# Mask passes of 32 rows beside the scores in a routed attention kernel

## The chip, the cores and the metric

The kernel runs on one core of a Trainium2 chip. A core has TensorE (PE in the profile), VectorE (DVE), ScalarE (ACT), GpSimd (POOL) and a queue for transfers (SP). The metric is the device time of one execution in microseconds; here the median of three runs.

## The reference

Two blocks follow each other: attention in which a query sees only the keys of its own cluster, and a two-layer network on the result. Only the first block is touched.

```python
q_assign = np.argmax(np.einsum('bhsd,hcd->bhsc', q_n, c_n), axis=-1)
k_assign = np.argmax(np.einsum('bhsd,hcd->bhsc', k_n, c_n), axis=-1)
mask = q_assign[:, :, :, None] == k_assign[:, :, None, :]
scores = scale * np.matmul(q, k.transpose(0, 1, 3, 2))
scores = np.where(mask, scores, -1000000000.0)
scores = scores - np.max(scores, axis=-1, keepdims=True)
attn = np.exp(scores)
attn = attn / (np.sum(attn, axis=-1, keepdims=True) + 1e-09)
return np.matmul(attn, v).astype(np.float32)
```

Batch 4, 8 heads, 768 tokens, head width 64, 16 clusters. The second block is `(h * erf(softplus(h))) @ w_out` with `h = x @ w_in`, for 3072 tokens, widths 512 and 2048.

## The kernel before

**Pairs, periods, units.** Attention goes through 16 pairs of heads (pair 0 to 15). The two heads `e` of a pair lie in partitions 0 to 63 and 64 to 127, so that two matmuls with 64 rows each work beside each other. A pair has 12 units `u`: two halves of 384 queries, and in each half six blocks of 128 keys. Two units make a period: six periods `i` = 0 to 5 for a pair, the first half in 0 to 2, the second in 3 to 5. `period(p, i)` writes out by hand the order of everything; every engine keeps the program's order (`InOrder`).

**What a unit needs.** `products` writes q times k in f32 into a `sc` bank (two pairs of passes, from `qT` and `kT`, in every third pair from parts of `more_out`). `scores` adds a bf16 pass of `km` and `qm`: the mask, and in one row the negative maximum of each query. `curve` is ACT's exponential from `sc` to `pr`. In the period after, `accumulate` sums `pr` on POOL and `attend` multiplies it with v into `turned[half]` (tile `turned`, 128 rows and 64 columns for each head).

**Masks.** `hotT` holds a one for each token's cluster. `masks(p, nm, half, bank)` multiplies it with the constant `pick`, which puts the 16 cluster rows of head `e` at the rows `e * 64` of a `turned` bank; ACT copies the bank to `qm` (Relu) or `km` (scale 2^60 and bias `nbig`, so that 0 stands where clusters agree and -2^60 elsewhere). The masks of the next pair are made in four places of a period's list (`MASKS`): place 0 after the first maxima step, 1 after the products, 2 after the scores with ACT's copy between the two curves, 3 at the end. Rows in use for a head: 16 cluster rows, and row 32 (`SH`) for the maximum.

**Maxima, half a pair ahead.** `maxima_step` finds the maxima for six units later: a pass of `qv` and `kv` (bf16 copies) into the one tile `wide`, a pass of `qm` and `km` on top, both with 64 rows, then a DVE reduction to `nmx`. A period has two such steps: at its start, and after the products. After every sixth step a small reduction writes `lowest`; at the start of periods 0 and 3 `turn` brings it to rows by six matmuls into `turned`, and ACT copies one row for each head into `qm` (`CAST qm<-turned`), which `scores` of that period reads.

**Other work in the order.** At the end of periods 0 and 3 `divide` multiplies the sums with `minus` on PE and takes `inv` on ACT; in the next period DVE makes `den` and `turned<-turned,inv` after place 0, and `more_out<-den,turned` after place 1, whose result SP stores. ACT makes the bf16 copies `kv` in period 4 and `qv` in period 5. For the second block DVE, ACT and POOL also rearrange weights in pairs 1 to 11 (`size_and_rest`, `bounded`, `sign`, `shifted`, `summed`; `sign` is the int16 `x_own` of the profile, in periods 2 and 4), and from pair 11 on DVE forms sums of weights. `similarities` and `choose`, for the pair after the next, begin in period 3 and end in 5.

The helper `InOrder` issues all instructions, so that nearly every row of the profile has the line L63; tiles tell the rows apart.

Of the kernel before, what the change touches and what calls it, by code (L numbers as in the profile page):

```python
# [20 lines left out]
B, H, S, D = 4, 8, 768, 64  # L21
C = 16
NJ = S // P
Q = 32
# [4 lines left out]
NPAIR = B * HP  # L29
# [14 lines left out]
BIG = 2.0**60  # L44
FLOOR = 2.0**50
EPS = 2.0**-70
SH = 2 * C
NPT = NJ + 2
N_LATE = 10
LAST_X = 11  # L50
MASKS = {(0, 1): ("k", 0), (0, 2): ("k", 1), (2, 0): ("q", 0), (5, 0): ("q", 1)}
FIRST_MASKS = {(2, 0): ("k", 0), (2, 1): ("q", 0), (2, 2): ("k", 1), (5, 0): ("q", 1)}


class InOrder:
# [16 lines left out]
def kernel(  # L72
# [13 lines left out]
    te, ve, ae, ge = (  # L86
        InOrder(tc, e, in_order) for e in (nc.tensor, nc.vector, nc.scalar, nc.gpsimd)
    )
# [8 lines left out]
    turned = [ps.tile([P, 512], F32, name=f"turned{i}") for i in range(2)]  # L97
# [12 lines left out]
    def passing(name, bufs, **kw):  # L110
        return attention.enter_context(tc.tile_pool(name=name, bufs=bufs, **kw))

    ps_s = passing("ps_s", 2, space=PSUM)
    wide = passing("ps_w", 1, space=PSUM).tile([P, 2, 512], F32, name="wide")
# [9 lines left out]
    first = const.tile([P, P], BF16, name="first")  # L124
    pick = const.tile([P, 2, P], BF16, name="pick")
    nbig = const.tile([P, 1], F32, name="nbig")
    ccT = const.tile([P, HP, 2 * C], F32, name="ccT")

    lowest = [const.tile([P, HJ, P], BF16, name=f"lowest{i}") for i in range(2)]
# [11 lines left out]
    rows = [{nm: const.tile([P, S], F32, name=f"{nm}T{i}") for nm in "qk"} for i in range(2)]  # L141
# [56 lines left out]
    for base, pattern, sign, op, fill in (  # L198
# [5 lines left out]
            out=first, in_=first, compare_op=op, fill=fill, base=base, pattern=pattern,  # L204
# [23 lines left out]
    steps = {}  # L228
# [29 lines left out]

    ve.memset(nbig, 0.0)
    for e in range(2):  # L260
        ve.memset(nbig[e * D : e * D + C], -BIG)
        ve.memset(nbig[e * D + SH : e * D + SH + 1], 1.0)
    for t in maxima:
        ve.memset(t, FLOOR)
    ve.memset(pick, 0.0)
# [81 lines left out]
        if p < NPAIR:  # L347
            ae.copy(out=pairs[p][nm + "v"], in_=pairs[p][nm + "T"])

    def masks(p, nm, half, bank):  # L350

        if p >= NPAIR:
            return lambda: None
        st = pairs[p]
        cols = slice(half * HW, (half + 1) * HW)
        r = slice(0, D) if nm == "q" else slice(D, P)
        won = bank[:, 0:HW]
        te.matmul(won, lhsT=pick[r, half], rhs=st["hotT"][r], start=True, stop=True)
        if nm == "q":
            return lambda: ae.activation(out=st["qm"][:, cols], in_=won, func=ACT.Relu)  # L360
        return lambda: ae.activation(
            out=st["km"][:, cols], in_=won, func=ACT.Identity, bias=nbig, scale=BIG
        )

    turns = []

    def maxima_step(p, i, sm=wide):

        st = pairs[p]
        nmx = maxima[p % 2]  # L370
        t, half = divmod(i, 2)
        for a, b, start in (("qv", "kv", True), ("qm", "km", False)):
            for e in range(2):
                r = slice(e * D, (e + 1) * D)
                te.matmul(
                    sm[:, e, 0:HW], lhsT=st[a][r, t * P : (t + 1) * P],
                    rhs=st[b][r, half * HW : (half + 1) * HW], start=start, stop=not start,
                )
        ve.tensor_reduce(
            out=nmx[:, :, t, half], in_=sm[:, :, 0:HW], axis=AX.X, op=ALU.max, negate=True  # L380
        )
        if i in (NJ - 1, 2 * NJ - 1):
            h = i // NJ
            ve.tensor_reduce(
                out=lowest[h][:, :, SH::D].rearrange("p t e -> p e t"),
                in_=nmx[:, :, h * HJ : (h + 1) * HJ], axis=AX.X, op=ALU.min,
            )
            turns.append((p, h))

    def turn(p, h, copies=(ae.copy, ae.copy)):  # L390

        st = pairs[p]
        pn = turned[h][:, 0:HW].rearrange("p (t n) -> p t n", t=HJ)
        for t in range(HJ):
            for e in range(2):
                cols = slice(e * D, (e + 1) * D)
                te.matmul(pn[cols, t], lhsT=lowest[h][:, t, cols], rhs=identb, start=True, stop=True)
        for e, copy in zip(range(2), copies):
            r = slice(e * D + SH, e * D + SH + 1)
            copy(out=st["qm"][r, h * HW : (h + 1) * HW], in_=pn[r].rearrange("p t n -> p (t n)"))  # L400
        st["shift", h] = True

# [20 lines left out]
    def scores(u):  # L423

        p, half, j = units[u]
        st = pairs[p]
        sc = sc_of[u]
        assert ("shift", half) in st
        for e in range(2):
            r = slice(e * D, (e + 1) * D)  # L430
            te.matmul(
                sc[:, e, 0:HW], lhsT=st["km"][r, j * P : (j + 1) * P],
                rhs=st["qm"][r, half * HW : (half + 1) * HW], start=False, stop=True,
            )
# [270 lines left out]
    def run(work):  # L705
        for _ in work:
            pass

    def step_ahead(u):
        p, i = divmod(u + NJ, 2 * NJ)
        if p < NPAIR:
            maxima_step(p, i)

    forms = sum((left_forms(ve, *w_in_parts(f, 2)) for f in range(0, HF, 2)), [])
    routing = [iter(())]
# [2 lines left out]
    def period(p, i):  # L720
        u = 2 * NJ * p + 2 * i
# [3 lines left out]
        def mask(place):  # L725
            which = (MASKS if p else FIRST_MASKS).get((i, place))
            if which:
                return masks(p + 1, *which, turned[0 if i in (0, 5) else 1])
            return lambda: None

        if u > 0:
            for which in turns if i in (0, 3) else ():
                turn(*which)
                turns.remove(which)
            step_ahead(u)
# [4 lines left out]
        products(u)  # L740
        products(u + 1)
        mask(1)()
        if u > 0:
            step_ahead(u + 1)
        next(part[0], None)
        scores(u)
        scores(u + 1)
        later = mask(2)
        if i == 3:
# [65 lines left out]
    def warm(n, bank, rhs):  # L815
        for _ in range(n):
            te.matmul(bank[:, 0 : rhs.shape[-1]], lhsT=identb, rhs=rhs, start=True, stop=True)
# [9 lines left out]
    for e in range(2):  # L827
        ve.tensor_copy(
            out=ccT[e * D : (e + 1) * D, :, e * C : (e + 1) * C],
            in_=pct[e * D : (e + 1) * D].rearrange("d (r e c) -> d r e c", e=2, c=C)[:, :, e],  # L830
# [7 lines left out]
    for r in (0, D):  # L838
        for half in range(2):
            for e in range(2):  # L840
                c = r + half * Q + e * C
                ve.tensor_copy(
                    out=pick[r : r + D, half, e * D : e * D + C], in_=first[r : r + D, c : c + C]
                )
    also = ps_s.tile([P, 2, 512], F32, name="sc", tag="s")
    products(0)
# [11 lines left out]
    for n in range(PLACES - 1):  # L858
        fetch(n)
    for i in range(NJ):  # L860
        maxima_step(0, i, also if i % 2 else wide)
        if i == 1:
            masks(0, "q", 1, turned[1])()
        if i < NJ - 1:
            warm(2, turned[0], zeros)
    step_ahead(0)
    warm(2, turned[0], zeros)
    turn(0, 0, (ae.copy, ve.tensor_copy))
    turns.clear()
    transposes(1, "k")  # L870
# [12 lines left out]
    u = len(units)  # L883
# [107 lines left out]
```

## Time and profile before

| what | value |
| --- | --- |
| median of three runs | 1022.77 us (1022.52 to 1022.77) |
| the execution profiled | 1022.77 us, of it span 1021.1 us from the first to the last instruction |
| granted TensorE clock | 1.00 |
| first `kv` pass, last score pass of the attention | 12.1 us, 433.6 us |
| PE busy from 50 to 400 us | 349.75 of 350.00 us |
| DVE, ACT, POOL busy from 50 to 400 us | 264.19, 266.40, 259.88 us |
| pair 8, period 1, `kv` to `kv` | 233.51 to 237.33 us |
| reduction `nmx<-wide` | 189 times, median 959 ns |
| ACT copies `qm<-turned` of 384 columns, 128 rows | 31 times, median 490 ns |
| ACT copies `km<-turned` | 32 times, mean 578 ns |

A row of the timeline gives start and duration in microseconds, engine, line, operation, output and inputs, rows times columns of a matmul's weights, shapes and number of instructions; idle time before it and who ended that stand in brackets. A matmul's duration includes its way through the array, so that two that follow each other overlap, and the distance of their starts tells the time that one takes.

### The profile page before, as it was taken

The page shows a single profiled execution, that of the slowest core. Times are in us where ns is not written, and L with a number is a line of the kernel's source. Part 1 is how long each engine was busy: PE and PEld are TensorE (multiplying, and loading weights), DVE is VectorE, ACT ScalarE, POOL GpSimd, SP SyncE. Part 2 cuts the span into 40 slices and gives each one's busy share as a digit, 9 for nine tenths or more (in the row PEclk, how much of TensorE's full clock was granted, in tenths as well). Part 3 has the DMA queues.
Part 4 walks back from the last instruction along what each step waited for, and adds up shares of the span by engine and source line. Part 5 has one row for each costly group of instructions (what it writes and reads, how often), then busy time and mean ns, then how long its engine had stood idle before and what let it go on. Part 6 is the DMA issues. An engine that isn't in the chain of part 4 may idle for free.

```text
span 1021.1 us, 15464 instructions
## 1 busy us (share of the span) xinstructions
PE 1013.9 (99%) x5930; PEld 726.1 (71%) x5930; DVE 695.8 (68%) x1305; ACT 515.0 (50%) x673; POOL 345.7 (34%) x229
## 2 busy tenths in 40 slices
PE   8999999999999999999999999999999999999998
PEld 3555555554555445478888888888888888888887
DVE  8777777777777777778875674756565547565754
ACT  3787877787777666567615142322233141505050
POOL 1777777777777667745130000000000000000000
PEclk9999999999999999999999999999999999999999
DMA  9344444444343311041100100110011000000001
GB/s 214 68 98 97 104 104 103 104 104 104 83 104 87 76 28 32 24 154 61 42 1 21 63 1 1 42 42 1 1 41 42 1 21 22 1 1 21 21 1 41
DMA packets 141641, 55.55 MB, mean 54 GB/s; under 512 B 127104, under 2 KB 131456, under 8 KB 141568
## 3 DMA queue, kind: packets, MB, share of 16 engines
q1 hardware_dynamic: 139216, 54.28, 20.8%
q8 instruction: 46, 0.75, 0.3%
q10 hardware_dynamic: 2352, 0.30, 0.2%
q14 instruction: 27, 0.22, 0.1%
HBM read 41.98 MB, written 12.58 MB: 53 GB/s over the span
## 4 chain that ended last, share of the span: by engine, by line
PE 97%; DVE 1%; POOL 0%; ACT 0%; issue 0%; DVEq 0%; ACTq 0%; POOLq 0%
PE bank L63 43%; PE turned L63 33%; PE sc L63 15%; PE wide L63 7%; DVE nmx L63 1%; POOL more_out L63 0%; DVE sims L63 0%; ACT inv L63 0%; DVE kT L63 0%; DVE qT L63 0%; ACT pr L63 0%; DVE hotT L63 0%; DVE wide L63 0%; DVE den L63 0%; DVE hot L63 0%
## 5 line engine op out<-in xcount | busy, mean ns | idle before, releaser
L63 POOL TENSOR_TENSOR more_out<-more_out,pr 128x768 f32<-128x768 f32 x128 | 223.5, 1746 | 67.6 <-ACT pr L63 62.5
L63 DVE TENSOR_REDUCE nmx<-wide 128x2 f32<-128x768 f32 x189 | 180.7, 956 | 95.1 <-PE wide L63 70.8
L63 ACT ACTIVATE pr<-sc 128x768 f32<-128x768 f32 x192 | 147.0, 810 | 75.0 <-PE sc L63 75.0
L63 PE MATMUL turned<-pr,in_v 128*64 128x386 f32 x768 | 145.5, 500 | 0.1
L63 DVE TENSOR_TENSOR g<-bank,g 128x256 f32<-128x256 f32 x222 | 89.5, 421 | 52.9 <-PE bank L63 46.3
L63 PE MATMUL bank<-x_own,w_in 128*128 128x256 f32 x424 | 104.5, 380 | 0.0
L63 PE MATMUL bank<-w_out,g 128*128 128x256 f32 x448 | 103.1, 379 | 0.0
L63 PE MATMUL sc<-qT,kT 64*128 64x384 f32 x528 | 99.7, 484 | 0.0
L63 PEld LDWEIGHTS turned<-pr,in_v 128*64 128x64 f32 x768 | 46.7, 136 | 72.2 <-issue 71.1
L63 PEld LDWEIGHTS bank<-w_out,g 128*128 128x128 f32 x448 | 85.2, 190 | 11.5
L63 PEld LDWEIGHTS bank<-x_own,w_in 128*128 128x128 f32 x424 | 80.4, 190 | 12.1 <-issue 1.2
L63 ACT COPY g<-bank 128x256 f32<-128x256 f32 x28 | 10.4, 372 | 152.5 <-PE bank L63 148.5
L63 DVE TENSOR_TENSOR osb<-bank,osb 128x256 f32<-128x256 f32 x87 | 35.4, 420 | 72.8 <-ACT osb L63 25.4
L63 ACT ACT_TABLE_LOAD x48 | 61.6, 1283 | 45.7 <-DVE g L63 45.0
L63 POOL TENSOR_TENSOR more_out<-pr,pr 128x768 f32<-128x768 f32 x32 | 58.8, 1837 | 58.5 <-ACT pr L63 58.5
L63 PE MATMUL bank<-x_more,more_in 128*128 128x256 f32 x296 | 76.0, 379 | 0.0
L63 PEld LDWEIGHTS <-qv 64*128 64x128 bf16 x384 | 25.6, 93 | 65.2 <-issue 51.1
L63 PE MATMUL wide<-kv,qv 64*128 64x384 bf16 x378 | 69.4, 328 | 1.1 <-ACT km L63 0.6
L63 PEld LDWEIGHTS sc<-qT,kT 64*128 64x128 f32 x528 | 56.6, 187 | 16.6 <-issue 1.2
L63 PE MATMUL wide<-km,qm 64*128 64x384 bf16 x378 | 68.3, 322 | 0.0
L63 PE MATMUL bank<-more_out,g_more 128*128 128x256 f32 x272 | 64.3, 379 | 0.0
L63 DVE TENSOR_TENSOR g<-a_s,g 128x512 f32<-128x512 f32 x96 | 62.4, 688 | 1.4 <-ACT a_s L63 1.4
(162 smaller groups left out, 1710.2 us busy)
## 6 DMA issues: line engine op xcount, KB each, us to landing
x_own<-in_moe_w_in_dram SPq DMA_DIRECT2D x13, 512.0 KB, 4.3
in_v<-in_v_dram SPq DMA_DIRECT2D x32, 192.0 KB, 2.9
x_dram<-more_out SPq DMA_DIRECT2D x32, 192.0 KB, 2.4
x_own<-x_dram SPq DMA_DIRECT2D x6, 1024.0 KB, 5.1
out_dram<-osb SPq DMA_DIRECT2D x23, 256.0 KB, 2.0
in_k<-in_k_dram SPq DMA_DIRECT2D x59, 96.0 KB, 2.7
in_q<-in_q_dram SPq DMA_DIRECT2D x58, 96.0 KB, 3.6
g_more<-in_moe_w_out_dram SPq DMA_DIRECT2D x6, 512.0 KB, 3.6
```

What stands on the lines that cost most here:

```text
L63: ins = getattr(self.engine, name)(*args, **kw)
```

## The change

The row of the maximum and the cluster rows move into 17 rows (row 0 the maximum, rows 1 to 16 the clusters), and `pick` writes them twice for each head: at rows 0 to 16 and at rows 32 to 48 of its 64, the second time with 0 for the maximum in `km`. `scores` now reads rows 0 to 31 of each head. `maxima_step` becomes a generator. The first step of a period runs through as before, with 64 rows. The second one stops after its `kv` pass (`behind`), is resumed after `scores(u)`, does its `km` pass with rows 32 to 63 of each head, and then its reduction. `next(part[0])`, the divide's second part, stands between the two. Two masks move: the second half of `k` from place 2 of period 0 to place 2 of period 2, the second half of `q` from place 0 to place 2 of period 5; in pair 0 the former was in that place already. At place 2 their product takes 32 rows of `hotT` and `pick` (`narrow`).

```diff
@@ -44,12 +44,11 @@
 BIG = 2.0**60
 FLOOR = 2.0**50
 EPS = 2.0**-70
-SH = 2 * C
 NPT = NJ + 2
 N_LATE = 10
 LAST_X = 11
-MASKS = {(0, 1): ("k", 0), (0, 2): ("k", 1), (2, 0): ("q", 0), (5, 0): ("q", 1)}
-FIRST_MASKS = {(2, 0): ("k", 0), (2, 1): ("q", 0), (2, 2): ("k", 1), (5, 0): ("q", 1)}
+MASKS = {(0, 1): ("k", 0), (2, 0): ("q", 0), (2, 2): ("k", 1), (5, 2): ("q", 1)}
+FIRST_MASKS = {(2, 0): ("k", 0), (2, 1): ("q", 0), (2, 2): ("k", 1), (5, 2): ("q", 1)}
 
 
 class InOrder:
@@ -258,8 +257,10 @@
 
     ve.memset(nbig, 0.0)
     for e in range(2):
-        ve.memset(nbig[e * D : e * D + C], -BIG)
-        ve.memset(nbig[e * D + SH : e * D + SH + 1], 1.0)
+        for n in range(2):
+            r = e * D + n * Q
+            ve.memset(nbig[r : r + C + 1], -BIG)
+            ve.memset(nbig[r : r + 1], 1.0 - n)
     for t in maxima:
         ve.memset(t, FLOOR)
     ve.memset(pick, 0.0)
@@ -347,13 +348,15 @@
         if p < NPAIR:
             ae.copy(out=pairs[p][nm + "v"], in_=pairs[p][nm + "T"])
 
-    def masks(p, nm, half, bank):
+    def masks(p, nm, half, bank, narrow=False):
 
         if p >= NPAIR:
             return lambda: None
         st = pairs[p]
         cols = slice(half * HW, (half + 1) * HW)
         r = slice(0, D) if nm == "q" else slice(D, P)
+        if narrow:
+            r = slice(r.start + half * Q, r.start + (half + 1) * Q)
         won = bank[:, 0:HW]
         te.matmul(won, lhsT=pick[r, half], rhs=st["hotT"][r], start=True, stop=True)
         if nm == "q":
@@ -364,25 +367,31 @@
 
     turns = []
 
-    def maxima_step(p, i, sm=wide):
+    def maxima_step(p, i, sm=wide, behind=False):
 
         st = pairs[p]
         nmx = maxima[p % 2]
         t, half = divmod(i, 2)
-        for a, b, start in (("qv", "kv", True), ("qm", "km", False)):
+
+        def passes(a, b, start, rows):
             for e in range(2):
-                r = slice(e * D, (e + 1) * D)
+                r = slice(e * D + rows.start, e * D + rows.stop)
                 te.matmul(
                     sm[:, e, 0:HW], lhsT=st[a][r, t * P : (t + 1) * P],
                     rhs=st[b][r, half * HW : (half + 1) * HW], start=start, stop=not start,
                 )
+
+        passes("qv", "kv", True, slice(0, D))
+        if behind:
+            yield
+        passes("qm", "km", False, slice(Q, D) if behind else slice(0, D))
         ve.tensor_reduce(
             out=nmx[:, :, t, half], in_=sm[:, :, 0:HW], axis=AX.X, op=ALU.max, negate=True
         )
         if i in (NJ - 1, 2 * NJ - 1):
             h = i // NJ
             ve.tensor_reduce(
-                out=lowest[h][:, :, SH::D].rearrange("p t e -> p e t"),
+                out=lowest[h][:, :, ::D].rearrange("p t e -> p e t"),
                 in_=nmx[:, :, h * HJ : (h + 1) * HJ], axis=AX.X, op=ALU.min,
             )
             turns.append((p, h))
@@ -396,7 +405,7 @@
                 cols = slice(e * D, (e + 1) * D)
                 te.matmul(pn[cols, t], lhsT=lowest[h][:, t, cols], rhs=identb, start=True, stop=True)
         for e, copy in zip(range(2), copies):
-            r = slice(e * D + SH, e * D + SH + 1)
+            r = slice(e * D, e * D + 1)
             copy(out=st["qm"][r, h * HW : (h + 1) * HW], in_=pn[r].rearrange("p t n -> p (t n)"))
         st["shift", h] = True
 
@@ -428,6 +437,7 @@
         assert ("shift", half) in st
         for e in range(2):
             r = slice(e * D, (e + 1) * D)
+            r = slice(r.start, r.start + Q)
             te.matmul(
                 sc[:, e, 0:HW], lhsT=st["km"][r, j * P : (j + 1) * P],
                 rhs=st["qm"][r, half * HW : (half + 1) * HW], start=False, stop=True,
@@ -708,10 +718,12 @@
 
 
 
-    def step_ahead(u):
+    def step_ahead(u, behind=False):
         p, i = divmod(u + NJ, 2 * NJ)
-        if p < NPAIR:
-            maxima_step(p, i)
+        steps = maxima_step(p, i, behind=behind) if p < NPAIR else iter(())
+        if not behind:
+            run(steps)
+        return steps
 
     forms = sum((left_forms(ve, *w_in_parts(f, 2)) for f in range(0, HF, 2)), [])
     routing = [iter(())]
@@ -725,7 +737,7 @@
         def mask(place):
             which = (MASKS if p else FIRST_MASKS).get((i, place))
             if which:
-                return masks(p + 1, *which, turned[0 if i in (0, 5) else 1])
+                return masks(p + 1, *which, turned[0 if i in (0, 5) else 1], place > 1)
             return lambda: None
 
         if u > 0:
@@ -740,10 +752,11 @@
         products(u)
         products(u + 1)
         mask(1)()
-        if u > 0:
-            step_ahead(u + 1)
+        second = step_ahead(u + 1, True) if u > 0 else iter(())
+        next(second, None)
         next(part[0], None)
         scores(u)
+        next(second, None)
         scores(u + 1)
         later = mask(2)
         if i == 3:
@@ -840,7 +853,8 @@
             for e in range(2):
                 c = r + half * Q + e * C
                 ve.tensor_copy(
-                    out=pick[r : r + D, half, e * D : e * D + C], in_=first[r : r + D, c : c + C]
+                    out=pick[r : r + D, half, e * D : (e + 1) * D].rearrange("p (n c) -> p n c", n=2)[:, :, 1 : C + 1],
+                    in_=first[r : r + D, c : c + C].unsqueeze(1).to_broadcast([D, 2, C]),
                 )
     also = ps_s.tile([P, 2, 512], F32, name="sc", tag="s")
     products(0)
@@ -858,7 +872,7 @@
     for n in range(PLACES - 1):
         fetch(n)
     for i in range(NJ):
-        maxima_step(0, i, also if i % 2 else wide)
+        run(maxima_step(0, i, also if i % 2 else wide))
         if i == 1:
             masks(0, "q", 1, turned[1])()
         if i < NJ - 1:
```

## The prediction

> **What bounds the kernel now.** I read the page first, then the PE's, ScalarE's (ACT) and VectorE's (DVE) parts of the timeline inside single periods of the attention part.
>
> ```profile
> PE 1013.9 (99%) x5930; PEld 726.1 (71%) x5930; DVE 695.8 (68%) x1305; ACT 515.0 (50%) x673; POOL 345.7 (34%) x229
> ```
>
> PE has no idle time to speak of, and the chain of waits gives it 97% of the span. But matmul ends are modelled, so lateness hides in start times. A period without masks, turns or divides before it (pair 8, period 1; the columns are start, duration, engine, line, operation):
>
> ```profile
> 233.51 0.34 PE L63 MATMUL wide<-kv,qv 64*128 64x384 bf16 x2
> ...
> 235.14 0.33 PE L63 MATMUL wide<-kv,qv 64*128 64x384 bf16 x2
> 235.30 0.33 PE L63 MATMUL wide<-km,qm 64*128 64x384 bf16 x2
> 235.46 0.49 PE L63 MATMUL sc<-qm,km 64*128 64x384 bf16 x4
> 235.88 1.52 PE L63 MATMUL turned<-pr,in_v 128*64 128x386 f32 x8
> 237.33 0.34 PE L63 MATMUL wide<-kv,qv 64*128 64x384 bf16 x2
> ```
>
> A pair of bf16 passes (two heads, one beside the other) takes one slot of 0.16 us; the period is 3.82 from `kv` to `kv`. From the second score slot (235.62) to the attend matmuls it is 0.26, not 0.16: 0.10 go with the change of tile shape. At the start 64-row passes at 14.20 are followed by 128-row ones at 14.46, again 0.26, though the columns stay 128. I read this as: a change of rows alone costs about 0.10 too.
>
> Period 0 of pair 9, whose beginning belongs to the turn:
>
> ```profile
> 254.66 0.34 PE L63 MATMUL turned<-identb,lowest 128*64 128x128 bf16 x6
> 254.94 0.34 PE L63 MATMUL wide<-kv,qv 64*128 64x384 bf16 x2
> ...
> 256.57 0.32 PE L63 MATMUL turned<-hotT,pick 64*128 64x384 bf16 x1
> ...
> 257.56 0.32 PE L63 MATMUL turned<-hotT,pick 64*128 64x384 bf16 x1
> 257.81 0.55 PE L63 MATMUL turned<-pr,in_v 128*64 128x386 f32 x2
> ```
>
> The last score pass here starts at 257.22; the second mask comes 0.34 after it, because it writes the bank that ACT is still copying the first mask from.
>
> ```profile
> 253.33 1.51 ACT L63 ACTIVATE pr<-sc 128x768 f32<-128x768 f32 x2 [0.21 <-PE sc L63]
> 254.73 0.83 ACT L63 CAST qv<-qT 128x768 bf16<-128x768 f32 x1
> 255.57 0.95 ACT L63 CAST qm<-turned 1x384 bf16<-1x384 f32 x2
> ...
> 258.19 0.58 ACT L63 ACTIVATE km<-turned,nbig 128x384 bf16<-128x384 f32 x1
> 258.65 0.81 ACT L63 ACTIVATE pr<-sc 128x768 f32<-128x768 f32 x1
> ```
>
> ACT runs from the curves of period 5 without a gap to the turn's two copies, which end at 256.52; the first mask starts at 256.57. **This queue is only just in time.** Between periods 2 and 3 it is late already:
>
> ```profile
> 239.87 1.51 ACT L63 ACTIVATE pr<-sc 128x768 f32<-128x768 f32 x2 [0.96 <-PE sc L63]
> 241.27 1.37 ACT L63 ACTIVATE x_own<-x_own 128x512 int16<-128x512 f32 x1
> 242.67 0.96 ACT L63 CAST qm<-turned 1x384 bf16<-1x384 f32 x2
> ```
>
> The copies end at 243.63, and the four score passes of that period (from 243.43) take 0.74 against the 0.49 above: 0.25 lost. DVE in period 1:
>
> ```profile
> 234.05 0.96 DVE L63 TENSOR_REDUCE nmx<-wide 128x2 f32<-128x768 f32 x1 [1.01 <-PE wide L63]
> 234.93 0.55 DVE L63 SCALAR_TENSOR_TENSOR den<-turned,inv 128x384 f32<-128x384 f32 x1
> 235.39 0.62 DVE L63 SCALAR_TENSOR_TENSOR turned<-turned,inv 128x384 f32<-128x384 f32 x1
> 235.92 0.95 DVE L63 TENSOR_REDUCE nmx<-wide 128x2 f32<-128x768 f32 x1
> 236.78 0.55 DVE L63 SCALAR_TENSOR_TENSOR more_out<-den,turned 128x384 f32<-128x384 f32 x1
> ```
>
> Five instructions back to back; the second reduction ends at 236.87 and frees `wide` for the `kv` at 237.33, 0.46 to spare.
>
> **What PE gains, step by step.** The second maxima step lies in 92 of 96 periods. Its mask pass moves beside the first scores: minus one slot, 0.16. The scores now take 32 rows, so between `kv` (64 rows) and scores there is a new change of shape: +0.10. It is not shown for 64 to 32 rows; bounds are 0 (as between passes of one shape) and 0.15 (scores to attend, 0.10, and 0.05 more of the first attend slot, 0.37 against 0.32). I take 0.10, the row with equal columns: net -0.06 x 92 = -5.5. Four periods have scores but no second step: +0.4. That four row tiles run at once the trace doesn't show, only two; bounds: free, or a whole slot of 0.16. The nearest row are the similarities, four column tiles started within 0.02 us and gone in 0.35, no more than the 0.37 of a two-tile attend slot after its change of shape: I take free.
>
> The Trainium skill, "TensorEngine Tiling (Array Packing)", Key Properties, says that changing the tiling mode drains TensorE; it gives no price. By the rule the change pays at each such border, as in the sum; without it the 92 slots would bring 14.7. Its "TensorE: Matmul & The Clock Gate", section "Measured speedup vs the span model", measured 3.07 times, not 4, for four 32-row tiles; an estimate from that page is a slot longer by a third, 0.05, some +2 us in all.
>
> Masks: in pairs 1 to 14 the second `k` mask leaves period 0, whose 0.34 and whose slot go together (scores to attend would be 0.25 again, against 257.22 to 257.81): -0.34 x 14 = -4.8. It goes beside scores in period 2, as does pair 0's, and the second `q` mask in period 5 of 15 pairs. A mask takes one head's rows alone and shifts it by a slot until the next change of shape: 16 x -0.16 = -2.6. What hides these masks is the second scores slot; without it 30 x 0.16 = 4.8 come back. PE alone: -5.5 + 0.4 - 4.8 - 2.6 = **-12.5**.
>
> **What the queues take.** *DVE, periods 1 and 4.* The change resumes the second step after the divide's last part, so `more_out<-den,turned` goes ahead of the second reduction. It reads the result before it: 235.39 + 0.62 + 0.03 (such a step in the similarity chain, 245.09 + 0.58 to 245.70) = 236.04, that is 2.53 after `kv`. The reduction follows 0.46 later (the spacing of `den`), runs 0.96, and PE needs 0.05 (copies' end to mask): 4.00, against 3.76 by PE alone. Next `kv` late by 0.24; 30 such places (period 1 of 15 pairs, period 4 of 15): +7.2. The reduction also comes 0.15 later against the next period everywhere; elsewhere 0.3 or more remains, except in pairs 12 and 13, where extra DVE sums lie between (there a reduction ends at 348.70 and `kv` starts at 348.75): +0.3.
>
> *ACT, period 5 into 0.* The `q` copy (0.49) was made before the curves, while ACT waited for scores; now it lies between them. From the scores' start: 0.43 to the curve, 1.40 for two curves, 0.39 for the copy (0.49 less the 0.10 by which such instructions overlap), 0.84 `qv`, 0.95 turn copies, 0.05: 4.06. PE reaches the first mask in 0.16 + 0.26 + 1.34 (attends) + 0.28 (turn) + 1.63 = 3.67. Late by 0.39, and second `kv`, scores and the attends are queued behind the mask: 14 x 0.39 = +5.5.
>
> *ACT, period 2 into 3.* The `k` copy is now between those curves (0.46, 258.19 to 258.65), ahead of the weight step `x_own` (1.40) in pairs 1 to 11: 0.43 + 1.40 + 0.46 + 1.40 + 0.96 + 0.05 = 4.70 to the scores of period 3. PE: 2.04 to `kv`, 1.63 + 0.26 to the scores, 3.93. Late by 0.77, of which 0.25 is there now: 11 x 0.52 = +5.7. Behind the scores wait the mask pass, similarities and attends. Without `x_own` the chain is 3.30, nothing late.
>
> *Setup.* Four more small memsets (59 ns each) on DVE and wider `pick` copies, partly under the centroids' load: 0 to 0.4, I take +0.2. No DMA is added; the store of `x` leaves one reduction earlier, SP waits on nothing new. POOL's sums get a later curve by 0.4 in periods 2 and 5, with over 1 us before the divide: nothing.
>
> Sum: -12.5 + 7.2 + 0.3 + 5.5 + 5.7 + 0.2 = **+6.4**. On the execution profiled (span 1021.1, timed 1022.77, which is the median shown): **1029.2 us**.
>
> **Rivals.** *No price from 64 to 32 rows.* Then -0.10, but only where PE decides: periods 1 and 4 wait for DVE, 3 for ACT; left are some 50 places, -5.0: 1024.2. For it: no row shows that border; against: both borders shown cost the same 0.10.
>
> *The change doesn't do what it says: 32-row passes run one after the other.* Then 0.16 per period, hidden again in 1 and 4 (0.24 of slack), and once each in the two ACT chains: some 36 places, +5.8: 1035.0. For: never seen here; against: the four column tiles.
>
> *Faster: ACT swallows the two copies.* One mechanism: between curves they cost ACT's queue nothing, as it idles elsewhere (50% busy, 0.96 idle before the curves of period 2). Then the 11.2 of both chains go: 1018.0. It decides for faster once the copies cost less than 0.37 of their 0.85 per pair. Against: 258.19 to 258.65 shows such a copy holding the next curve by 0.46, and the idle time lies before the curves, where the copy no longer is.
>
> **Numbers.** Forecast 0.64; no price 0.10 (half of it above +0.2%); one after the other 0.14; faster 0.09; something cancelling within 0.2% 0.03. A time within 0.2% (2.0 us) is no change that a measurement here can tell. Faster 0.09, same 0.08, slower 0.83. The forecast's own range is 1026 to 1032 (drain 0.05 to 0.15 in some 50 places); with most of both neighbours 1024.6 to 1034.6.
>
> **What would show it.** After: `kv` to `kv` in periods 1 and 4 about 4.00, with `more_out<-den,turned` ahead of the second `nmx`; scores 0.26 after the second `kv`, the narrow `km` within 0.01 of the scores and the next scores 0.16 on; no mask after the scores of period 0; the first mask there late by 0.4 behind the turn copies; scores of period 3 late by 0.8. Wrong: `kv` to `kv` at 3.76 or less in period 1, or a mask in period 0 that starts 1.63 after `kv`.

## The result, and the profile after

| | median | lowest to highest | runs |
| --- | --- | --- | --- |
| before | 1022.68 us | 1022.52 to 1022.77 | 5 |
| after | 1051.19 us | 1051.17 to 1052.42 | 5 |

The changed kernel takes 1.0281 times as long, with an interval of 1.0269 to 1.0292: **28.5 us slower**, where the prediction had 6.4 and a range that ended at 1034.6. The sign was right, the size was not. The execution profiled is the one of 1052.42 us (span 1050.7), 29.65 above the profile of before.

First the page's busy times and its chain of waits, of the kernel after:

```profile
PE 1009.8 (96%) x5930; PEld 705.2 (67%) x5930; DVE 736.6 (70%) x1309; ACT 511.0 (49%) x673; POOL 342.2 (33%) x229
...
PE 70%; DVE 25%; DMA 3%; issue 1%; ACT 0%; SPq 0%; DVEq 0%
```

The chain of before:

```profile
PE 97%; DVE 1%; POOL 0%; ACT 0%; issue 0%; DVEq 0%; ACTq 0%; POOLq 0%
```

PE has 4.1 us less to do, in a span that is 29.6 longer. VectorE is busy for 40.8 us more, with four instructions more, and its share of the chain that ended last goes from 1% to 25%. Which wait that is, says the list of PE's waits (who waits, for whom, us in all, times, longest), of after:

```profile
PE wide L62 <- DVE nmx L62: 31.0, 60, 1.6
```

and of before:

```profile
PE wide L63 <- DVE nmx L63: 0.4, 2, 0.2
```

Sixty times a `kv` pass waits for a reduction to free `wide`. From the starts of the first `kv` pass of every period, the lengths of the periods of pair 8 (pairs 1 to 11 agree within 0.03 us) against those that the prediction's terms give (period 0: 4.97 - 0.06 - 0.34 + 0.39; period 3: 5.50 - 0.06 + 0.52; period 5: 4.15 - 0.06 - 0.16):

| period | 0 | 1 | 2 | 3 | 4 | 5 |
| --- | --- | --- | --- | --- | --- | --- |
| before | 4.97 | 3.82 | 4.15 | 5.50 | 3.82 | 4.15 |
| predicted | 4.96 | 4.00 | 4.09 | 5.96 | 4.00 | 3.93 |
| after | 5.49 | 4.01 | 4.09 | 6.81 | 4.01 | 3.93 |

Four of six are right to 0.01. Periods 0 and 3 are 0.53 and 0.85 too long. A pair is longer than before by 1.96 us in pairs 1 to 11 (21.5 in all), and by 4.15, 2.46, 0.76 and 1.13 in pairs 12 to 15, mostly in periods 0 and 3 again (in pair 14 in period 3 alone).

The timeline of TensorE after, a period without turns or masks (pair 7, period 4; columns as in the lines of before):

```profile
235.52 0.34 PE L62 MATMUL wide<-kv,qv 64*128 64x384 bf16 x2
235.80 0.34 PE L62 MATMUL sc<-qm,km 32*128 32x384 bf16 x2
235.80 0.33 PE L62 MATMUL wide<-km,qm 32*128 32x384 bf16 x2
235.97 0.32 PE L62 MATMUL sc<-qm,km 32*128 32x384 bf16 x2
236.22 1.52 PE L62 MATMUL turned<-pr,in_v 128*64 128x386 f32 x8
237.92 0.34 PE L62 MATMUL wide<-kv,qv 64*128 64x384 bf16 x2 [0.17 <-DVE nmx L62]
```

Everything that the change wanted of PE is here: scores and the narrow `km` pass start together, the next scores 0.17 later. The last line is the wait that was predicted for periods 1 and 4. What was not predicted stands in period 0, here of pair 8:

```profile
241.85 0.34 PE L62 MATMUL wide<-kv,qv 64*128 64x384 bf16 x2
...
243.73 0.32 PE L62 MATMUL turned<-hotT,pick 64*128 64x384 bf16 x1
244.55 0.34 PE L62 MATMUL wide<-kv,qv 64*128 64x384 bf16 x2 [0.50 <-DVE nmx L62]
```

The mask starts 1.88 after `kv`, 0.25 later than in the sum for PE alone. Yet the second `kv` does not follow it by a slot; it starts 0.82 behind the mask, held by the first reduction. VectorE over the same stretch, after:

```profile
241.22 0.18 DVE L62 TENSOR_REDUCE lowest<-nmx 128x6 bf16<-128x18 f32 x1
241.31 1.85 DVE L62 TENSOR_SCALAR w_in<-w_in 128x512 f32<-128x512 f32 x1
243.08 0.57 DVE L62 STREAM_TRANSPOSE hotT<-hot 128x384 bf16<-128x384 bf16 x1
243.58 0.92 DVE L62 TENSOR_REDUCE nmx<-wide 128x2 f32<-128x768 f32 x1
```

and before, at the same place of pair 8:

```profile
254.10 0.18 DVE L63 TENSOR_REDUCE lowest<-nmx 128x6 bf16<-128x18 f32 x1
254.19 0.42 DVE L63 TENSOR_SCALAR w_out<-w_out 128x512 f32<-128x512 f32 x1
254.52 0.57 DVE L63 STREAM_TRANSPOSE hotT<-hot 128x384 bf16<-128x384 bf16 x1
255.48 0.96 DVE L63 TENSOR_REDUCE nmx<-wide 128x2 f32<-128x768 f32 x1 [0.38 <-PE wide L63]
```

The order is the same. One instruction, the maximum over a weight tile that `bounded` issues in place at the ends of periods 2 and 5, takes **1.85 us in the place of 0.42**, on the same shape. Everything behind it is late, and the reduction at 243.58, which before idled 0.38 waiting for PE, is now what PE waits for. The rows by tile (ns: shortest, median, longest) show how general that is. The group of before, and then that of after:

```profile
L63 DVE TENSOR_SCALAR w_in<-w_in x32: 415/417/419, 43.1 to 244.5; 128x512 f32<-128x512 f32 x16, 128x512 uint32<-128x512 uint32 x16
L62 DVE TENSOR_SCALAR w_in<-w_in x32: 416/1134/1867, 42.9 to 260.1; 128x512 f32<-128x512 f32 x16, 128x512 uint32<-128x512 uint32 x16
```

Half of these 32 rows are `bounded`; taken with those on `w_out` there are 22, and after all 22 take 1.85 to 1.87. What else ran then? GpSimd, before, in the stretch of the lines above:

```profile
254.29 3.61 POOL L63 TENSOR_TENSOR more_out<-more_out,pr 128x768 f32<-128x768 f32 x2 [0.54 <-ACT pr L63]
```

and after:

```profile
241.20 3.50 POOL L62 TENSOR_TENSOR more_out<-more_out,pr 128x768 f32<-128x768 f32 x2 [0.26 <-ACT pr L62]
```

Before, VectorE's maximum starts at 254.19, 0.10 us **ahead** of GpSimd's running sum at 254.29. After, it starts at 241.31, 0.11 **behind** the sum at 241.20. A row joins two sums here; singly, the first takes 1.86 before and 1.68 after. The rows singly, for all 22 places: before, 20 of the maxima start 0.09 to 0.10 ahead and two 0.38 and 0.45; after, all 22 start 0.11 behind.

### The profile page after: what moved, and what is told of

The parts are those of the page before. It is cut to its first block, busy times and chain, and to the rows that moved or that the text cites. A ratio compares the mean times of both kernels' runs of the same rounds, so it can differ in the third digit from the quotient of the medians.

```text
span 1050.7 us, 15481 instructions
## 1 busy us (share of the span) xinstructions
PE 1009.8 (96%) x5930; PEld 705.2 (67%) x5930; DVE 736.6 (70%) x1309; ACT 511.0 (49%) x673; POOL 342.2 (33%) x229
## 4 chain that ended last, share of the span: by engine, by line
PE 70%; DVE 25%; DMA 3%; issue 1%; ACT 0%; SPq 0%; DVEq 0%
PE bank L62 42%; PE turned L62 19%; DVE nmx L62 11%; PE sc L62 5%; PE wide L62 4%; DVE w_in L62 3%; DVE more_out L62 2%; DMA x_dram<-more_out 2%; DVE turned L62 2%; DVE den L62 1%; DMA in_q<-in_q_dram 1%; DVE w_out L62 1%; DVE more_in L62 1%; DVE kT L62 1%; DVE sims L62 1%
## 5 line engine op out<-in xcount | busy, mean ns | idle before, releaser
L62 POOL TENSOR_TENSOR more_out<-more_out,pr 128x768 f32<-128x768 f32 x128 | 220.0, 1718 | 73.1 <-ACT pr L62 67.1
L62 PEld LDWEIGHTS <-qv 64*128 64x128 bf16 x384 | 30.5, 93 | 102.3 <-issue 87.8
L62 PE MATMUL wide<-kv,qv 64*128 64x384 bf16 x378 | 65.6, 327 | 32.7 <-DVE nmx L62 31.0
L62 PEld LDWEIGHTS sc<-qT,kT 64*128 64x128 f32 x528 | 53.1, 187 | 19.1 <-ACT pr L62 1.2
L62 PE MATMUL wide<-km,qm 64*128 64x384 bf16 (+1 forms) x378 | 63.0, 327 | 0.0
```

Of the source, the lines that this page charges most:

```text
L62: ins = getattr(self.engine, name)(*args, **kw)
```

## The experiments

**The theory.** Of the two instructions the one that starts second is held until the first is through: VectorE's from the sum's start to 0.28 after its end (0.11 + 1.85 = 1.96 = 1.68 + 0.28), or GpSimd's by 0.18. The change flipped the order, because the curve that releases GpSimd follows the scores, and the reduction ahead of `lowest` and `bounded` follows the mask pass. That pass was made one slot before the scores, and is now made beside them. The rows of that reduction (DVE) show the shift: before, in period 2 of pair 8, it starts 0.22 us ahead of the first curve (ACT, at 239.87),

```profile
239.65 0.96 DVE L63 TENSOR_REDUCE nmx<-wide 128x2 f32<-128x768 f32 x1 [0.82 <-PE sc L63]
```

and after, in the same period, 0.02 ahead of it:

```profile
253.80 0.96 DVE L62 TENSOR_REDUCE nmx<-wide 128x2 f32<-128x768 f32 x1 [0.95 <-PE wide L62]
253.82 0.81 ACT L62 ACTIVATE pr<-sc 128x768 f32<-128x768 f32 x1 [1.14 <-PE wide L62]
```

**The rival**: the narrow tiles, or the wider reach of the change, cost something themselves, and the maximum's length is a sign of it.

### The maximum moved out of the sum's way

```diff
-        elif i == 2 and early(n1):
-            bounded(n1)
             sign(n1)
         elif i == 3:
             if early(n1):
+                bounded(n1)
                 shifted(n1)
...
+            bounded(n1 - 1)
             shifted(n1 - 1)
...
-        elif i == 5 and early(n2):
-            bounded(n2)
```

> The kernel after, with VectorE's in-place maximum on a weight tile (bounded, 512 columns) taken out of periods 2 and 5 and put before the shift of the same tile in the next period, 3 or 0, where GpSimd has no sum running. Theory A (in periods 2 and 5 of the kernel after, GpSimd's sum starts 0.11 us ahead of this instruction, which then runs 1.85 us instead of 0.42 and delays the next reduction and the kv pass behind it): no such instruction over 0.5 us in pairs 1 to 11, period 0 falls from 5.49 to about 5.0 us and period 3 from 6.81 to about 5.9, together 11 x (0.5 + 0.9) = 15: about 1036 us. Theory B (the excess over the prediction comes from the two mask copies on ScalarE, or from the narrow tiles on TensorE): the periods keep their lengths, about 1051 us.

Measured: 1038.30 us, 1.0157 times before (1.014 to 1.0174): 12.9 of the 28.5 are gone. Period 0 of pair 8 falls from 5.49 to 4.81. Period 3 falls from 6.81 only to 6.32, though the maximum is short there. TensorE and then VectorE in that period:

```profile
250.64 1.52 PE L62 MATMUL turned<-pr,in_v 128*64 128x386 f32 x8
252.23 0.87 PE L62 MATMUL turned<-more_out,minus 128*64 128x384 f32 x4
253.32 0.34 PE L62 MATMUL wide<-kv,qv 64*128 64x384 bf16 x2 [0.23 <-DVE hot L62]
```

```profile
249.84 0.96 DVE L62 TENSOR_REDUCE nmx<-wide 128x2 f32<-128x768 f32 x1 [1.33 <-PE wide L62]
250.72 0.88 DVE L62 TENSOR_SCALAR w_in<-w_in 128x512 f32<-128x512 f32 x2
251.51 0.57 DVE L62 STREAM_TRANSPOSE sims<-turned 128x384 f32<-128x384 f32 x1
```

The maximum and the shift now lie ahead of the transpose that empties the bank of the similarities; the divide's matmuls write that bank and begin at 252.23, behind it. So the experiment takes one stall away and adds a smaller one, of some 0.4 us in each of 11 periods (from the first of these attends to the next `kv` it is 2.68 us, against 2.25 in the changed kernel). It shows that the maximum's place decides; the size is told apart by the next two.

### The kernel before, with the order flipped

Nothing of the change in it: five idle one-column memsets ahead of the maximum in periods 2 and 5.

```diff
-    def bounded(n):
+    def bounded(n, late=0):
         w = w_steps[n][0]
+        for _ in range(late):
+            ve.memset(idle, 0.0)
         ve.tensor_scalar(out=w, in0=w, scalar1=2.0, scalar2=None, op0=ALU.max)
...
-            bounded(n1)
+            bounded(n1, 5)
...
-            bounded(n2)
+            bounded(n2, 5)
```

> The kernel before, no narrow tile in it, with five memsets of one column (0.06 us each) on VectorE ahead of the same instruction in periods 2 and 5, so that it comes some 0.2 us behind GpSimd's sum and not 0.1 us ahead of it. Theory A: it runs about 1.6 to 1.9 us, the first reduction of the next period comes about 1.5 us later, and periods 0 and 3 of pairs 1 to 11 grow by 1.1 to 1.3 us each: about 1049 us (1042 to 1052). Theory B: VectorE is late by 0.3 us only, for which the trace shows room: 1022.7 to 1024 us.

Measured: 1046.83 us, 1.0236 times before (1.0221 to 1.0252). VectorE, and then GpSimd, in this version of the kernel before:

```profile
257.51 0.46 DVE L63 MEMSET idle<- 128x1 f32 x4
258.01 1.52 DVE L63 TENSOR_SCALAR w_in<-w_in 128x512 f32<-128x512 f32 x1
```

```profile
257.57 3.50 POOL L63 TENSOR_TENSOR more_out<-more_out,pr 128x768 f32<-128x768 f32 x2 [0.54 <-ACT pr L63]
```

The maximum starts 0.44 behind the sum and takes 1.52: again it ends 1.96 after the sum's start. With half a microsecond of idle memsets the kernel before is 24.2 us slower; its periods 0 and 3 go from 4.97 and 5.50 to 5.71 and 6.74, the others stay. Of the 24.2, 22.5 lie in pairs 1 to 11; another 1.4 lie ahead of the first `kv` pass (13.57 us instead of 12.14), where VectorE waits for the loads of q and k in this profile, and have nothing to do with the order. **The rival falls**: the stall needs no narrow tile.

### The changed kernel, with the order flipped back

The maximum is issued one instruction earlier, ahead of the small `lowest` reduction (0.18 us); `first_of_all` hands the weight tile's number to the second step. All else is the changed kernel.

```diff
+        while behind and first_of_all:
+            bounded(first_of_all.pop())
         if i in (NJ - 1, 2 * NJ - 1):
             h = i // NJ
             ve.tensor_reduce(
                 out=lowest[h][:, :, ::D].rearrange("p t e -> p e t"),
...
-            bounded(n1)
...
-            bounded(n2)
```

> The kernel after with two neighbours on VectorE exchanged: in periods 2 and 5 the weight tile's maximum (bounded) runs ahead of the small reduction to lowest and not behind it, so that it starts about 0.1 us ahead of GpSimd's sum instead of 0.11 us behind it. Theory A (who starts first decides): 0.42 us each, GpSimd's sum takes 1.86 us and not 1.68, periods 0 and 3 of pairs 1 to 11 fall by some 0.6 and 0.95 us: about 1034 us (1032 to 1037). Theory B (the order of the two is worth their own 0.1 to 0.3 us): 1050 to 1052 us.

Measured: 1033.30 us, 1.0102 times before (1.0085 to 1.0119): two neighbours on VectorE's queue changed places, and **17.9 us** are back. VectorE, and then GpSimd, in it:

```profile
243.08 0.42 DVE L62 TENSOR_SCALAR w_in<-w_in 128x512 f32<-128x512 f32 x1
243.41 0.18 DVE L62 TENSOR_REDUCE lowest<-nmx 128x6 bf16<-128x18 f32 x1
```

```profile
243.17 3.61 POOL L62 TENSOR_TENSOR more_out<-more_out,pr 128x768 f32<-128x768 f32 x2 [0.72 <-ACT pr L62]
```

Again 0.09 ahead, and 0.42 long. Period 0 of pair 8 takes 4.70, period 3 5.76; periods 2 and 5 give 0.09 and 0.11 of it back, as `lowest`, and with it the turn, comes later.

### The divide's last part behind the second reduction

The first experiment with `next(part[0], None)` after the second step's resumption:

```diff
         next(second, None)
-        next(part[0], None)
         scores(u)
         next(second, None)
+        next(part[0], None)
         scores(u + 1)
```

> As e1, and the divide's last part on VectorE is issued behind the second reduction again, not ahead of it. Prediction's term (periods 1 and 4 wait for VectorE, 0.24 us in each of 30 places): kv to kv in periods 1 and 4 falls from 4.01 to about 3.77, 7 us less than e1: about 1029 us. Rival (something else holds these periods at 4.01, the narrow tiles for instance): the time of e1.

Measured: 1030.79 us, 1.0079 (1.0064 to 1.0094), that is 7.5 less than the version that it starts from. Periods 1 and 4 are 3.76 instead of 4.01: the term of +7.2 for VectorE is shown, and with it 3.82 - 0.06, PE's own gain. With VectorE out of the way, ACT's chains can be read here. ACT at the end of period 2 of pair 8, behind the two curves with the `k` mask's copy between them:

```profile
243.22 1.37 ACT L62 ACTIVATE x_own<-x_own 128x512 int16<-128x512 f32 x1
244.31 1.06 ACT L62 CAST qm<-turned 1x384 bf16<-1x384 f32 x2
```

The scores started at 240.93, the copies end at 245.37, and the next period's scores go on at 245.42: a chain of 4.49, predicted 4.70. The copy of the turn starts 1.09 after the weight step, not 1.40.

### The masks back where they were

The version just described with the lists `MASKS` (shown) and `FIRST_MASKS` of the kernel before.

```diff
-MASKS = {(0, 1): ("k", 0), (2, 0): ("q", 0), (2, 2): ("k", 1), (5, 2): ("q", 1)}
+MASKS = {(0, 1): ("k", 0), (0, 2): ("k", 1), (2, 0): ("q", 0), (5, 0): ("q", 1)}
```

> As e3, and the masks in the four places of the kernel before (second k mask in period 0 behind the first one, second q mask in period 5 before the products). Prediction's terms: ScalarE's chains into periods 0 and 3 lose 0.39 and 0.52 us (14 x 0.39 + 11 x 0.52 = 11.2), TensorE gets the masks back (14 x 0.34 + 15 x 0.16 = 7.2): 4 us less than e3, about 1025 us, period 3 at about 5.4. Rival (ScalarE swallows the copies): e3 lies at about 1018 and this one 7 us above it.

Measured: 1031.26 us, 1.0083 (1.0068 to 1.0098): 0.5 more, not the 4 less that were expected. Period 3 falls by 0.44 (expected 0.52), but periods 0 and 5 rise by 0.15 and 0.16, and a weight sum of pair 14 now meets GpSimd's sum (its period 0 rises from 4.81 to 5.90). Moving the two masks is close to free as it stands: in pairs 1 to 11 it costs 0.44 a pair by ACT's queue and saves 0.31 on PE.

### The weight work behind the routing

The version with the divide's last part behind the second reduction (1030.79 us), with the maximum, the shift and, from pair 12 on, the weight sums (VectorE's two-input sums of 128 x 512) moved behind `choose` in period 3. No sum is left in period 2 or 5 of pairs 11 to 14.

```diff
+    12: {0: 1, 3: 2}, 13: {0: 1, 3: 2}, 14: {0: 2, 3: 4}, 15: {0: 1, 2: 1, 3: 2, 4: 2, 5: 2},
...
         if i == 3:
             for _ in range(3):
                 next(routing[0], None)
+            if early(n1):
+                bounded(n1)
+                shifted(n1)
```

> As e3, but the maximum and the shift of the weight tile follow choose's steps in period 3 (in e3 they stood ahead of its transpose, which the divide's matmuls wait for), and the sums of weights in pairs 11 to 14 are moved out of periods 2 and 5 into 0 and 3, where GpSimd is idle. Theory A: period 3 of pairs 1 to 11 falls by about 0.4 us, periods 0 and 3 of pairs 12 and 13 from 5.75 and 6.92 to about 4.8 and 5.2: 4.4 + 5.5 less than e3, about 1021 us (1019 to 1024). Theory B (these periods are long through the narrow tiles or ScalarE): the time of e3, 1030.8.

Measured: 1028.54 us, 1.0061 (1.0046 to 1.0076), 2.2 less than the version that it starts from, and 7.5 more than expected. Period 3 falls from 6.31 to 5.73 in pairs 1 to 11, and periods 0 and 3 of pairs 12 and 13 from 5.75 and 6.92 to 4.81 and 5.19: the moved sums had made these long. But period 4 rises from 3.76 to 4.37, in pairs 12 to 14 by 1.0 to 2.8. VectorE, and then GpSimd, in pair 8:

```profile
248.21 0.55 DVE L61 TENSOR_TENSOR hot<-sims,wide 128x384 bf16<-128x384 f32 x1
248.68 1.50 DVE L61 TENSOR_SCALAR w_in<-w_in 128x512 f32<-128x512 f32 x2
250.10 0.95 DVE L61 TENSOR_REDUCE nmx<-wide 128x2 f32<-128x768 f32 x1
```

```profile
247.59 1.84 POOL L61 TENSOR_TENSOR more_out<-pr,pr 128x768 f32<-128x768 f32 x1 [1.67 <-ACT pr L61]
```

Behind the routing GpSimd's next sum already runs (247.59 to 249.43). The two steps, 0.88 long in the first experiment, take 1.50, and the reduction at 250.10 is late. The `hot` comparison, which runs beside the same sum, is not held and keeps its 0.55; one of its two inputs lies in `wide`, a bank that TensorE writes. The expectation had taken VectorE's durations as fixed once more.

The same with other masks, chosen so that no copy lies between the curves ahead of a turn:

```diff
-MASKS = {(0, 1): ("k", 0), (2, 0): ("q", 0), (2, 2): ("k", 1), (5, 2): ("q", 1)}
+MASKS = {(0, 2): ("k", 1), (2, 0): ("q", 0), (2, 1): ("k", 0), (5, 0): ("q", 1)}
```

> As e5, with the masks placed so that ScalarE's copies keep out of the way: only the second k mask in period 0, narrow and beside the scores; q and then k in period 2 ahead of the scores, one on each head's rows; the second q mask in period 5 before the products. ScalarE's terms then go and two masks pair up: period 0 0.39 less, period 3 0.44 less in pairs 1 to 11, period 5 0.16 more: 8 less than e5, about 1013 us (1010 to 1016). If the prediction's ScalarE terms are no part of the time, e6 is within 2 us of e5.

Measured: 1024.42 us, 1.001 (1.0001 to 1.0019). Six of its ten runs, at 1024.4 to 1024.5, have a mean granted clock of 0.998, the other four, at 1022.3 to 1022.9, one of 1.00. Period 3 falls from 5.73 to 5.29 and period 5 rises by 0.16, as expected; period 0 falls from 4.81 to 4.57, by 0.24 where 0.39 was expected. Period 4 keeps the stall of the version that it starts from, whose own miss of 7.5 is the larger part of the 11.4 by which the expected 1013 is missed.

### Together, and its controls

The maximum ahead of `lowest`, the divide's part later, these masks, and the weight sums in fewer periods, in period 3 behind the routing.

```diff
-    11: {5: 1}, 12: {0: 1, 2: 1, 5: 1}, 13: {0: 1, 2: 1, 5: 1}, 14: {0: 2, 2: 1, 3: 1, 5: 1},
-    15: {0: 1, 2: 1, 3: 2, 4: 2, 5: 2},
+    12: {0: 1}, 13: {0: 1}, 14: {0: 2, 3: 2}, 15: {0: 2, 2: 2, 3: 3, 4: 3, 5: 4},
```

> The narrow passes of the kernel after, with all that the runs so far point to: the maximum ahead of the small reduction (as e7), the divide's last part behind the second reduction (as e3), the masks placed as in e6, and the sums of weights kept to periods in which neither GpSimd nor a reduction waits for them (one in period 0 of pairs 12 and 13, two each in 0 and 3 of pair 14, the rest in pair 15). By the periods measured in those runs, 4.57 + 3.76 + 4.17 + 5.3 + 3.76 + 4.19 = 25.75 for pairs 1 to 11 against 26.39 in the kernel before, 0.8 less in the other pairs: about 1012 us (1010 to 1016), faster than the kernel before. Rival (the narrow passes cost something that these periods don't show): not under 1020.

Measured: **1016.28 us**, 0.9937 of before (0.9924 to 0.9951), 6.4 us faster than the kernel before and 34.9 faster than the changed one. Its periods in pair 8 are 4.57, 3.76, 4.20, 5.35, 3.76 and 4.19. The list of PE's waits, of this version:

```profile
PE wide L61 <- DVE nmx L61: 0.5, 3, 0.2
```

From 31.0 back to 0.5. It stays 4.3 above the expected 1012. 1.2 of this is period 4 of pair 15, which takes 5.07 from scores to scores, where the changed kernel has 3.87: there three sums lie on VectorE that meet GpSimd's. Another 0.5 lie behind the last scores, and pairs 1 to 11 take 25.85 on average, not 25.75.

The control is the kernel before with nothing but these other places for the sums.

> The kernel before with nothing but the sums of weights moved as in e8: a control. Both theories: within 1.5 us of the kernel before, since only one reduction there waits for such a sum (by 0.1 to 0.2 us in pairs 12 and 13).

Measured: 1024.67 us, 1.0019 (1.0011 to 1.0028): the sums' places cost 2.0 us on their own (period 4 of pair 15, from scores to scores, goes from 3.41 to 4.50, and the time behind the last scores grows by as much), so the gain of 6.4 does not come from them. The other masks' places and the maximum's place were not tried without the narrow passes; what share of the 6.4 is theirs stays open.

Two attempts to draw the sums forward, the first with two each in periods 0 and 3 of pairs 12 and 13, three each in those of pair 14, and none in periods 4 and 5 of pair 15:

> The version before it (together, 1016.28 us) with the twenty weight sums drawn forward: two each in periods 0 and 3 of pairs 12 and 13, three each in periods 0 and 3 of pair 14, three, one and two in periods 0, 2 and 3 of pair 15, none in its periods 4 and 5. Theory (a sum costs nothing where it lies clear of GpSimd's running sum, and over a microsecond where it starts behind one): period 4 of pair 15 falls from 5.07 to about 3.5 and the tail by 0 to 1.5; periods 3 of pairs 12 and 13 stay at 5.19 if the sums end before GpSimd's next one starts, else +0.6 each in period 4. 1014.0 us, 1012.5 to 1016.0. Rival (the sums need their time on VectorE wherever they lie): within 0.5 of 1016.28.

Measured: 1021.89 us, 0.9991 (0.9982 to 1.0), 5.6 more than without it. The second, without the two in period 3 of pairs 12 and 13:

> As the one beside it, but nothing in period 3 of pairs 12 and 13; pair 15 takes three, two, three and two sums in periods 0, 2, 3 and 5. Theory: pairs 12 and 13 as in the version of 1016.28; period 4 of pair 15 about 3.5 to 4.5, the tail as there or 0.5 better. 1014.8 us, 1013.5 to 1016.3. Rival (the sums need their time wherever they lie): within 0.5 of 1016.28.

Measured: 1021.08 us, 0.9989 (0.998 to 0.9998). Both miss both of their theories. VectorE, and then GpSimd, of the first one, at the start of pair 14:

```profile
384.78 0.68 DVE L61 TENSOR_TENSOR more_in<-w_in 128x512 f32<-128x512 f32 x1
385.49 0.69 DVE L61 TENSOR_TENSOR more_in<-more_in,w_in 128x512 f32<-128x512 f32 x1
386.10 2.31 DVE L61 TENSOR_TENSOR w_in<-w_in 128x512 f32<-128x512 f32 x1
```

```profile
385.98 1.88 POOL L61 TENSOR_TENSOR more_out<-pr,pr 128x768 f32<-128x768 f32 x1 [1.62 <-ACT pr L61]
```

The first two sums start ahead of GpSimd's, by 1.20 and 0.49, and keep their length; the third starts 0.12 behind and takes 2.31. The period that follows is 5.34 instead of 3.76. Period 4 of pair 15 did fall to 3.87 in the first attempt, against some 3.5 expected (in the second it is 5.21), but the three third sums in pairs 14 and 15 cost 1.6 each in both, and the two in period 3 of pairs 12 and 13 another 1.0 a pair in the first. That the order of the starts decides holds in both; the fault was to count free time on VectorE and not to look where GpSimd's next sum starts.

## Why the prediction was wrong

**The step that failed** is the sentence at the end of VectorE's part: the reduction "also comes 0.15 later against the next period everywhere; elsewhere 0.3 or more remains". The prediction lets a lateness of 0.15 pass through the instructions behind the reduction with their lengths of before, and finds room for it. But the first large instruction behind it stood 0.10 us ahead of a GpSimd sum that holds it if it comes second. The lateness of one slot did not add 0.15, it added 1.43 (1.85 for 0.42), twice in a pair; PE sees what is left of it after VectorE's slack. In pairs 1 to 11 the excess over the forecast is 0.53 + 0.85 in periods 0 and 3, about 15 us for the eleven; in pairs 12 to 15 the weight sums are held in the same way (0.68 becomes 2.1), some 8 us more in the profiled execution (1.7 of it TensorE's clock, see the end). Together that is the missing 22 to 23. The version of the kernel before with the memsets and the one of the changed kernel with the two neighbours exchanged show it from both sides, with one instruction's place: 22.5 us more in pairs 1 to 11 of the one, 17.9 less in the other.

It was to be seen. GpSimd was weighed once, and only for its own sums' being late. And VectorE's rows of before had held instructions of three times their length, in pair 15:

```profile
423.50 0.68 DVE L63 TENSOR_TENSOR more_in<-more_in,w_in 128x512 f32<-128x512 f32 x1
424.10 2.17 DVE L63 TENSOR_TENSOR w_in<-w_in 128x512 f32<-128x512 f32 x1
```

with GpSimd's rows beside them:

```profile
423.59 4.21 POOL L63 TENSOR_TENSOR more_out<-more_out,pr 128x768 f32<-128x768 f32 x2 [0.39 <-ACT pr L63]
```

The same operation on the same shape takes 0.68 where it starts 0.09 ahead of the sum and 2.17 where it starts while the sum runs.

The Trainium skill, "SBUF — State Buffer", section "Who interferes with whom", says that VectorE and GpSimd share one pair of ports under an exclusive lock, that whichever of them issues first has it for the whole instruction and the other blocks, and that on VectorE this concerns, among others, `tensor_scalar` in its two-port modes and instructions with two inputs in SBUF. The runs agree, in both kinds (0.42 to 1.85, 0.68 to between 2.1 and 2.3), and in who goes first; in which mode the maximum ran, no profile here says. The prediction did not draw on it.

**The other steps.**

- *PE's gains* were right: periods 2 and 5 are 4.09 and 3.93 as summed. The new border from 64 to 32 rows costs 0.10, the value taken (median of 92 places: 0.27 from `kv` to scores, against 0.17 between passes of one shape), so the rival without a price falls. Four row tiles of 32 start within 0.01, and the next scores follow 0.17 later: no extra slot, so the rival of passes one after the other falls as well. The slot longer by a third, estimated from the 3.07 of "TensorE: Matmul & The Clock Gate" in the Trainium skill, section "Measured speedup vs the span model", is not seen: a slot keeps its 0.17.
- *VectorE in periods 1 and 4*: 4.01 against 4.00, and 3.76 once the divide's part is out of the way.
- *ACT from 5 into 0* was sized too large: 0.24 late where VectorE is clear (period 0 of 4.81 in the first experiment), not 0.39; the chain from scores to mask is 3.92, not 4.06.
- *ACT from 2 into 3* too: 0.44 (what returning the masks takes off), not 0.52; the chain is 4.49, not 4.70. In the changed kernel neither of the two lengthens a period: VectorE's longer lateness covers both.
- *The faster rival* (ACT swallows the copies) falls by the same two numbers.
- *Pairs 12 and 13*, where 0.3 was put for VectorE's extra sums: 0.78 in period 0 of each, and 3.25 (1.7 of it TensorE's clock) and 1.56 in their periods 3, by held sums.
- *Setup*: pair 0's first step begins 0.23 earlier, where 0.2 later had been summed; in the other versions with the same setup it begins 0.04 to 0.28 later than in the kernel before, so that one profile does not tell this term.

The undisturbed sum was near, and partly by luck: the kernel with the neighbours exchanged is at 1033.3. Its pairs 1 to 11 take 26.71 on average, where the terms give 26.94, and its pairs 12 to 15, with stalled sums still in them, are 6.8 longer than before, where next to nothing had been summed.

## What to carry to other kernels

An instruction's length in a profile holds only for its place beside the other engines: before a shift of a fraction of a microsecond is passed down a queue, look for each instruction behind it that starts just ahead of one of another engine with which it can collide, and price the flipped order, not the shift. Where one operation on one shape has two lengths in the rows of before, find out why first. In a tight schedule a neighbour's exchange may be worth more than the change itself.

## What the runs showed of the hardware

- VectorE against GpSimd, f32 in SBUF: a `tensor_scalar` of 128 x 512 takes 0.42 us alone or ahead; behind a `tensor_tensor` of GpSimd of 128 x 768 (1.68 us) it ends 0.28 us after that one's end, whether it came 0.11 or 0.44 behind it. GpSimd's own takes 1.86 when it comes 0.10 behind. So 1.43 us are lost on the one side or 0.18 on the other, by who is first.
- The blocked instruction is one long busy row in the trace, with no idle time before it and no releaser: VectorE seems to work harder (736.6 against 695.8 us), while it stands.
- TensorE's granted clock fell once in the changed kernel's profile. The windows of it (length in us; busy time and count of PE, its weight loads, DVE, ACT and POOL; granted clock, DMA share, GB/s):

```profile
372.00:374.00 2.00, 1.58 (x18) 0.47 (x19) 1.23 (x2) 0.85 (x2) 0.17 (x1) 1.00 0.69 111
374.00:376.00 2.00, 2.00 (x8) 0.81 (x10) 1.79 (x4) 0.67 (x1) 1.26 (x1) 0.50 0.59 94
376.00:378.00 2.00, 2.00 (x12) 0.56 (x10) 0.00 (x0) 0.20 (x1) 0.58 (x1) 0.65 0.00 0
```

  It comes some 1.5 us behind the end of a wait of TensorE of 1.55 us for `nmx`; period 3 of pair 12 takes 8.61 there, that of pair 13, with the same wait and the full clock, 6.92. The four other runs of the kernel are 1.2 to 1.3 us shorter and have a mean clock of 1.00, where the profiled one has 0.998. The same is seen in pair 14 of the version with the weight work behind the routing: behind a wait of 2.18 us its clock falls to 0.50 in one window of 2 us, and the version with other masks, with a wait of 2.19 there, keeps 1.00. What sets it off was not tried.
